# Second MLP: where the last factor's product, the first MLP's last matmuls and the second half's blocks stand in the queues

## The chip, the cores and the metric

One core of one Trainium2 chip. Five instruction queues run beside each other: TensorE (PE; its weight loads are listed as PEld), VectorE (DVE), ScalarE (ACT), GpSimd (POOL) and SyncE (SP), which only issues DMAs. Each queue works its own instructions strictly in the order of the program, and waits where one needs a result of another queue. The metric is the device time of one launch in microseconds; the median of the runs is given. One profiled execution stands beside them.

## The reference, cut to what matters

```python
x = attention(q, k, v)                    # windowed attention with block summaries, x is 1536 x 512
h = x @ w_in                              # first MLP, 512 -> 2048
y = (h * sigmoid(h)) @ w_out              # y is 1536 x 512
a = y @ w_a;  b = y @ w_b                 # second MLP, 512 -> 1536 each
out = (a * b) @ w_out2                    # 1536 x 512
```

Every large product is made of three matmuls on a high and a low part of each operand (high·high, high·low, low·high). The high part is a copy rounded to fp32r, the low part is the rest. So each operand costs one copy (on ACT in most places) and one subtraction (on DVE or POOL) before PE can use it.

## The kernel before, in words

The order of all instructions is written out by hand (`manual_schedule`); nothing is planned by costs. Attention and the first MLP run first, woven into each other. The change touches the passage from the first MLP to the second, and the second MLP.

**End of the first MLP.** A slot of the loop is `mm1` (h), `chain1` (silu and its two parts) and `mm2` of two slots before. When the loop ends, `mm2` of the last two slots is still to be done: eight calls `mm2_part(i, c)` of three matmuls each (L551). The last four finish the four pieces of y for tokens 1024 to 1535, and `keep_y` copies each from PSUM: pieces 0 and 2 on DVE, 1 and 3 on ACT.

**Second MLP.** Tokens are in two halves, q = 0 (tokens 0 to 767) and q = 1 (768 to 1535). The products y·w_a and y·w_b are done with a seven-product (Winograd) scheme on 2 x 2 blocks. A *unit* u is a pair of weight tiles, even u for w_a and odd u for w_b; a *pair* p is units 2p and 2p+1. Of y, each half needs seven blocks, each with a high part (`high_y`, an ACT copy 128x768) and a low part (`low_y`, 128x768): B11, B21 and B22 as they are, and T3 = B22 − B12, T1 = B12 − B11, T2 = T3 + B11, T4 = B21 − T2, which `sum_y` makes in place in the same buffers, so that T3 waits for the parts of B22, T2 overwrites B11 and waits for T1, and so on. For half 0 this is done within the loop; for half 1 the list `second_y` holds the 18 steps, each with its engine.

**A group.** `group(parts, chunks, fills, later)` walks through the seven `PRODUCTS` (k = 0 to 6), and for each k through its parts (unit, half, bank pair). One product is six matmuls of 384 columns (L750) into one of two PSUM banks A and B: k = 0, 2, 4, 6 go to A and k = 1, 3, 5 to B, and k = 2, 3, 5, 6 add onto what is there. After each product come, in this order: `after_product`, then the entries of `later` that are due, then `chunks`, then `fills` of that place in the group. The bank pair of the first part is called bankh in the trace, that of the second bankg. A product that writes a bank has to wait until the instruction that reads the bank's former content is done.

**after_product.** k = 0 copies A to t1 (ACT, L699); k = 1 and 3 make u2 and u3 from B and t1 (DVE, L701, L703). k = 2, 4, 5, 6 finish one of the four factor blocks `at`. For an even unit it is written (ACT L710 or DVE L712). For an odd unit it is multiplied: k = 2 in one instruction (DVE L715), the others with the *bank sum* `x = ps + x` (DVE, L718), which releases the bank, and then the product `at = x * at` (L719), on POOL for k = 4 and 5 and on DVE for k = 6. The rest goes to `later` with a number of products to wait: a DMA of the factor to DRAM (the spill, L725), and for half 0 the high part (`hi`, ACT L733), which in turn puts the low part (`lo`, DVE L737) two products later.

**Order of the groups.** First `[(0, 0, 0), (1, 0, 1)]`: units 0 and 1 of half 0, 14 products in alternation. Into its first places the eight `mm2_part` calls are put, two after each of the first four products, and `second_y` into places 4 to 13. Then nine output matmuls, then unit 0 of half 1 (7 products), then unit 1 of half 1. After that each unit u = 2 to 11 is one group of 14 products, half 0 and half 1 in alternation, with the output matmuls of the pair before (`mm5`, L775, named o in the trace) as chunks and the preparation of the next weights as fills. At places 0 and 1 of an even unit's group stand the two parts of two tiles of w_out2 (`high_wo2` on ACT, `low_wo2` on POOL, L495), which the output matmul at place 4 reads first. At the end `later` is emptied, the last pair's output matmuls follow, and then 288 output matmuls of the other row blocks (L796).

Of the kernel before, what the change touches and what calls it, by code (L numbers as in the profile page):

```python
# [14 lines left out]
ALU = mybir.AluOpType  # L15
# [66 lines left out]
def attention_then_two_mlps(ctx, tc, q, k, v, w_in, w_out, w_a, w_b, w_out2, out):  # L82
# [3 lines left out]
    nc = tc.nc  # L86
# [17 lines left out]
    TH = PT // 2  # L104
# [38 lines left out]
    engines = {"v": nc.vector, "p": nc.gpsimd}  # L143
# [505 lines left out]
    def weights(u, part, i, j):  # L649

        if u % 2:
            assert j == i + 1
            return beside[7 * part + i][:, None, :]
        if u not in wab_t:
            wab_t[u] = pools["w"].tile([P, 2, 7, 2 * P], F32R, tag="wab", name=f"wab{u}", bufs=1)
        return wab_t[u][:, part, i:j]
# [12 lines left out]
    def sum_y(q, name, engine):  # L669
        x, y, op = SUMS[name]  # L670
        engines[engine].tensor_tensor(y_of(q, name), y_of(q, x), y_of(q, y), op=op)
# [9 lines left out]
    def high_y(q, name, h):  # L681
        yc_t[q, name] = [h, None]
        nc.scalar.copy(h, y_of(q, name))

    def low_y(q, name, l, engine):
        h, x = yc_t[q, name][0], y_of(q, name)
        yc_t[q, name][1] = l
        engines[engine].tensor_tensor(l, x, h.bitcast(F32), op=ALU.subtract)

    def spill_of(f):  # L690
        if f not in spill_p:
            spill_p[f] = dram.tile([P, NDEF * P], F32, name=f"spp{f}")
        return spill_p[f]

    def after_product(u, k, q, n, later):
        p, w = divmod(u, 2)
        (A, B), (t1, u2, u3) = banks[n], post["t"][3 * n:3 * n + 3]
        if k == 0:
            nc.scalar.copy(t1, A)  # L699
        elif k == 1:  # L700
            nc.vector.tensor_tensor(u2, B, t1, op=ALU.add)  # L701
        elif k == 3:
            nc.vector.tensor_tensor(u3, B, t1, op=ALU.add)  # L703
        else:

            i, t, ps, x = {2: (0, 0, A, None), 4: (1, 1, A, u3), 5: (1, 0, B, t1), 6: (0, 1, A, u2)}[k]
            at = post["a"][4 * q + 2 * i + t]
            if w == 0:
                if x is None:
                    nc.scalar.copy(at, ps)  # L710
                else:
                    nc.vector.tensor_tensor(at, ps, x, op=ALU.add)  # L712
                return
            if x is None:
                nc.vector.tensor_tensor(at, ps, at, op=ALU.mult)  # L715
            else:

                nc.vector.tensor_tensor(x, ps, x, op=ALU.add)  # L718
                engines["v" if k == 6 else "p"].tensor_tensor(at, x, at, op=ALU.mult)  # L719
            f = 2 * p + i  # L720
            if q or t:

                c = slice(0 if q else P, TH)
                to = q * PT + t * TH + c.start - NOW * P
                later.append((2, lambda: nc.sync.dma_start(spill_of(f)[:, to:to + TH - c.start], at[:, c])))  # L725
            if not q:
                n = P if t else TH

                def hi():
                    if t and (p, "t") not in p_t:  # L730
                        p_t[p, "t"] = work.tile([P, 2, 2, P], F32R, tag="g", name=f"p{p}_t", bufs=3)
                    p_t[p, i, t] = p_t[p, "t"][:, i] if t else work.tile([P, 2, TH], F32R, tag="g", name=f"p{p}_{i}", bufs=3)
                    nc.scalar.copy(p_t[p, i, t][:, 0], at[:, 0:n])  # L733
                    later.append((2, lo))

                def lo():
                    nc.vector.tensor_tensor(p_t[p, i, t][:, 1], at[:, 0:n], p_t[p, i, t][:, 0].bitcast(F32), op=ALU.subtract)  # L737
                later.append((2 if k in (4, 5) else 1, hi))

    def group(parts, chunks, fills, later):  # L740


        at = 0
        for k, (s, y, b, more) in enumerate(PRODUCTS):
            for u, q, n in parts:
                A, B = banks[n]
                idx = 0
                for c in range(2):
                    for a, m in PARTS:
                        nc.tensor.matmul((A, B)[b], weights(u, a, s, s + 1)[:, 0, c * P:(c + 1) * P], yc_t[q, y][m][:, c, :],  # L750
                                         start=(idx == 0 and not more), stop=(idx == 5), skip_group_check=more)
                        idx += 1
                now = [f for x, f in later if x <= 1]
                later[:] = [(x - 1, f) for x, f in later if x > 1]
                after_product(u, k, q, n, later)
                for f in now + chunks.get(at, []) + fills.get(at, []):
                    f()
                at += 1
# [43 lines left out]
    with tc.manual_schedule():  # L802
# [128 lines left out]
        def high_2(name):  # L931
            return lambda: high_y(1, name, places.pop(0))

        def low_2(name, engine):
            return lambda: low_y(1, name, places.pop(0), engine)

        def sum_2(name, engine):
            return lambda: sum_y(1, name, engine)

        second_y = [high_2("B11"), high_2("B22"), low_2("B11", "v"), high_2("B21"), low_2("B22", "p"), sum_2("T3", "v"),  # L940
                    sum_2("T1", "p"), low_2("B21", "p"), sum_2("T2", "v"), high_2("T2"), high_2("T3"), low_2("T2", "v"),
                    sum_2("T4", "p"), high_2("T1"), low_2("T3", "v"), high_2("T4"), low_2("T1", "p"), low_2("T4", "p")]

# [12 lines left out]
        def call(f, *a):  # L956
            return lambda: f(*a)

        def spread(steps, first, last):

            r = {}
            for i, f in enumerate(steps):
                r.setdefault(first + i * (last - first + 1) // len(steps), []).append(f)
            return r

        def merged(*parts):
            r = {}
            for x in parts:
                for k, v in x.items():
                    r.setdefault(k, []).extend(v)  # L970
            return r

        def chunks_of(p):
            return [call(mm5, p, i, t) for i, t in ((0, 0), (0, 1), (0, 2), (1, 3), (1, 0), (1, 1), (1, 2), (0, 3))]
# [4 lines left out]
        def split_wo2(p):  # L979
            return [call(high_wo2, 2 * p), call(low_wo2, 2 * p)], [call(high_wo2, 2 * p + 1), call(low_wo2, 2 * p + 1)]  # L980
# [3 lines left out]
        later = []  # L984

        m2 = [call(mm2_part, i, c) for i in (SLOTS - 2, SLOTS - 1) for c in range(NK)]
        f0, f1 = split_wo2(0)
        group([(0, 0, 0), (1, 0, 1)], {0: m2[0:2], 1: m2[2:4], 2: m2[4:6], 3: m2[6:8]},
              merged({0: f0 + [call(load_unit, 2)], 1: f1}, spread(second_y, 4, 13)), later)
        c = chunks_of(0)  # L990
        for f in c[0:3]:
            f()
# [5 lines left out]
        for u in range(2, UNITS):  # L998
            p, w = divmod(u, 2)
# [5 lines left out]
            if w == 0:  # L1005
                c = chunks_of(p - 1) if p > 1 else []
                if p > 1:
                    f0, f1 = split_wo2(p - 1)
# [10 lines left out]
            else:  # L1019
                if dB is not None:  # L1020
                    parts.append({8: [call(decode_tile, dB)], 9: loads[3:4]})
                if p + 1 == PAIRS:
                    f0, f1 = split_wo2(p)
# [56 lines left out]
```

## Time and profile before

| | |
|---|---|
| runs | 642.73, 642.88, 644.02 us; median 642.88 us |
| profiled execution | 644.93 us, of which the span of the trace is 643.2 us |
| mean granted TensorE clock | 0.995 of full speed |
| PE busy | 615.2 us (96%), 3440 instructions |
| DVE, ACT, POOL busy | 409.0, 307.9 and 308.0 us (64%, 48%, 48%) |

Engine rows give the busy time and its share of the span. In a row of the timeline, the first number is the start in us from the span's start, the second the time from the start of the first to the end of the last instruction that the row merges, xN their count, and the bracket the idle time of that engine before it, with what ended it. Matmul ends are modelled: one of 384 columns is shown 0.33 us long, while the next one starts 0.17 us after it.

### The profile page before, as it was taken

Reading aid. Unit: us, or ns where it says so; the run is one execution under the profiler, and the core shown is the slowest. Engines: PE = TensorE matmul, PEld = TensorE weight load, DVE = VectorE, ACT = ScalarE, POOL = GpSimd, SP = SyncE. Lnnn points to the kernel's source line nnn. Section 1 sums busy time; section 2 is a strip of 40 time slices with the busy share of each in tenths; the row PEclk is TensorE's granted clock in tenths of the full one; section 3 lists DMA queues with packets and bytes.
Section 4 is the critical chain, followed back from the end, with each engine's and each line's share of the span. In section 5 each row is a group of like instructions: output and inputs, shape, how many; then the busy total and the mean of one; then the engine's idle time right before and its main releaser. Section 6 shows DMA issues by size and latency. Waiting matters only on the chain.

```text
span 643.2 us, 9778 instructions
## 1 busy us (share of the span) xinstructions
PE 615.2 (96%) x3440; PEld 537.6 (84%) x3440; DVE 409.0 (64%) x768; ACT 307.9 (48%) x680; POOL 308.0 (48%) x277
## 2 busy tenths in 40 slices
PE   6899999899999999999999889999999999999997
PEld 5888877788878888888888879989999998988886
DVE  6999878985752334567676774685867747364211
ACT  4999678848565224545555323242423324224221
POOL 5657666642431502334457556384654838154220
PEclk8999999899999999999999999999999999999999
DMA  9898998653230235675654013554362502258303
GB/s 230 187 228 246 296 269 255 189 162 103 76 74 18 75 99 170 223 217 177 197 196 167 29 50 103 172 168 148 118 210 83 196 28 88 77 180 305 131 12 130
DMA packets 90521, 97.80 MB, mean 152 GB/s; under 512 B 39000, under 2 KB 68440, under 8 KB 90472
## 3 DMA queue, kind: packets, MB, share of 16 engines
q1 hardware_dynamic: 90472, 97.18, 50.2%
q8 instruction: 27, 0.44, 0.3%
q14 instruction: 22, 0.18, 0.1%
HBM read 73.79 MB, written 23.07 MB: 151 GB/s over the span
## 4 chain that ended last, share of the span: by engine, by line
PE 79%; DVE 11%; ACT 6%; issue 2%; DMA 2%; POOL 0%; SPq 0%; ACTq 0%; DVEq 0%
PE y L551 18%; PE h L518 17%; PE bankg L750 12%; PE bankh L750 12%; PE ol L796 10%; PE o L775 4%; PE sc L360 2%; ACT sm L389 1%; PE av L423 1%; DVE p_t L737 1%; DVE ab L719 1%; DVE sum L718 1%; PE pt L409 1%; DMA sp_out<-w_out 1%; DVE u_in L468 1%
## 5 line engine op out<-in xcount | busy, mean ns | idle before, releaser
L518 PE MATMUL h<-x,w_in 128*128 128x512 f32 (+1 forms) x612 | 143.9, 385 | 0.7 <-DVE g L533 0.6
L551 PE MATMUL y<-g,w_out 128*128 128x512 f32 x576 | 141.3, 394 | 0.8 <-DVE w_out L495 0.8
L518 PEld LDWEIGHTS h<-x,w_in 128*128 128x128 f32 x612 | 110.0, 190 | 23.2 <-issue 0.8
L551 PEld LDWEIGHTS y<-g,w_out 128*128 128x128 f32 x576 | 106.8, 188 | 24.1 <-DVE w_out L495 1.3
L495 POOL TENSOR_TENSOR w_out<-re_out,w_out 128x512 fp32r<-128x512 f32 x37 | 52.1, 1409 | 116.1 <-ACT w_out L147 115.7
L796 PE MATMUL ol<-w_out,plh 128*128 128x512 f32 x192 | 59.1, 389 | 0.0
L533 DVE TENSOR_TENSOR g<-h,g 128x512 fp32r<-128x512 f32 x31 | 21.4, 691 | 49.6 <-ACT g L147 49.4
L495 POOL TENSOR_TENSOR w_out<-w_out,w_out 128x512 fp32r<-128x512 f32 x23 | 31.8, 1389 | 34.5 <-ACT w_out L147 31.0
L719 POOL TENSOR_TENSOR ab<-sum,ab 128x384 f32<-128x384 f32 x24 | 28.5, 1193 | 31.2 <-DVE sum L718 31.1
L526 ACT ACTIVATE h<-h 128x512 f32<-128x512 f32 x31 | 18.0, 582 | 51.1 <-PE h L518 51.1
L796 PEld LDWEIGHTS ol<-w_out,plh 128*128 128x128 f32 x192 | 36.0, 188 | 7.5
L533 POOL TENSOR_TENSOR g<-sg,g 128x512 fp32r<-128x512 f32 x17 | 24.4, 1438 | 36.3 <-ACT g L147 13.2
L147 ACT CAST w_out<-re_out 128x512 fp32r<-128x512 f32 x38 | 23.7, 623 | 34.1 <-issue 23.2
L796 PE MATMUL ol<-w_out,pll 128*128 128x512 f32 x96 | 37.3, 389 | 0.0
L788 DVE TENSOR_TENSOR pll<-pl,plh 128x1024 fp32r<-128x1024 f32 x12 | 17.0, 1416 | 30.9 <-ACT plh L787 30.9
L775 PE MATMUL o<-w_out,p 128*128 128x512 f32 x108 | 30.2, 396 | 0.5 <-DVE p L737 0.5
L403 POOL TENSOR_TENSOR sm<-sm,st 128x480 f32<-128x480 f32 x20 | 22.2, 1116 | 15.8 <-DVE st L399 9.7
L472 DVE SCALAR_TENSOR_TENSOR w_out<-w_out,u_out 128x512 uint32<-128x512 uint32 x28 | 27.3, 976 | 3.7 <-ACT w_out L462 2.3
L389 ACT ACTIVATE sm<-sm,st 128x120 f32<-128x120 f32 x76 | 29.1, 395 | 0.1
L495 POOL TENSOR_TENSOR w_in<-w_in,w_in 128x512 fp32r<-128x512 f32 x15 | 21.5, 1437 | 14.3 <-DVE w_in L149 8.1
L750 PE MATMUL bankh<-yhT,wab 128*128 128x384 f32 x96 | 28.2, 334 | 0.0
L639 POOL TENSOR_TENSOR wab<-c,wab 128x768 fp32r<-128x768 f32 x6 | 11.3, 1877 | 34.4 <-ACT wab L636 34.4
(262 smaller groups left out, 1431.3 us busy)
## 6 DMA issues: line engine op xcount, KB each, us to landing
st_out<-in_moe_w_out_dram SPq DMA_DIRECT2D x28, 512.0 KB, 4.6
re_out<-sp_out SPq DMA_DIRECT2D x44, 256.0 KB, 3.0
st_in<-in_moe_w_in_dram SPq DMA_DIRECT2D x16, 512.0 KB, 6.1
sp_out<-w_out SPq DMA_DIRECT2D x28, 256.0 KB, 2.1
st_a<-in_moe_w_a_dram SPq DMA_DIRECT2D x12, 512.0 KB, 4.0
st_b<-in_moe_w_b_dram SPq DMA_DIRECT2D x12, 512.0 KB, 4.1
c<-spu SPq DMA_DIRECT2D x12, 512.0 KB, 4.1
pl<-spp SPq DMA_DIRECT2D x12, 512.0 KB, 4.5
```

The source lines that it names most:

```text
L147: nc.scalar.copy(o, i)
L389: nc.scalar.activation(sm[:, pr, :], sm[:, pr, :], AF.Exp, scale=-1.0, bias=st[:, 0, pr:pr + 1], accum_out=st[:, 1, pr:pr + 1])
L403: engines[engine].tensor_tensor(sm, sm, st[:, 1, :, None].to_broadcast([P, NPR, KK]), op=ALU.mult)
L472: nc.vector.scalar_tensor_tensor(bits, bits, 3, u_t.pop((kind, f)), op0=ALU.logical_shift_left, op1=ALU.bitwise_or)
L495: engine.tensor_tensor(w[:, 1], w32_t[kind, f], w[:, 0].bitcast(F32), op=ALU.subtract)
L518: nc.tensor.matmul(h_ps[i][:, cols], win_t[f][:, a, c * P:(c + 1) * P], x_t[n][:, steps, m, c, :], start=(idx == 0), stop=(idx == 3 * NK - 1))
L533: engines[engine].tensor_tensor(g_t[i][:, 1], sg_t.pop(i), g_t[i][:, 0].bitcast(F32), op=ALU.subtract)
L551: nc.tensor.matmul(y_ps[n, c], wout_t[i][:, a, c * P:(c + 1) * P], g_t[i][:, m, :], start=(f == 0 and (a, m) == (0, 0)), stop=(f == N1 - 1 ...
L719: engines["v" if k == 6 else "p"].tensor_tensor(at, x, at, op=ALU.mult)
L750: nc.tensor.matmul((A, B)[b], weights(u, a, s, s + 1)[:, 0, c * P:(c + 1) * P], yc_t[q, y][m][:, c, :], start=(idx == 0 and not more), sto ...
L775: nc.tensor.matmul(o_ps[t], g[:, a, c:c + P], w[:, m], start=(begins and (a, m) == (0, 0)), stop=(ends and (a, m) == PARTS[-1]))
L796: nc.tensor.matmul(late_o[j], late_p[f][a][:, j * P:(j + 1) * P], wo2_t[N2 + f][:, m], start=(f == 0 and (a, m) == (0, 0)), stop=(f == N2 ...
```

## The change

The factor's product of k = 6 of an odd unit is put into `later` for one product instead of being issued at once. The spill is due after three products instead of two. `hi` of k = 6 is due after two products instead of one (k = 4 and 5 had two before, k = 2 keeps one). The low part of B22 of half 1 is made on DVE instead of POOL. The eight last `mm2_part` calls, the first two w_out2 tiles and the first step of `second_y` come ahead of the first group, and the other 17 steps of `second_y` are spread over its places 0 to 12.

```diff
@@ after_product
                 nc.vector.tensor_tensor(x, ps, x, op=ALU.add)
-                engines["v" if k == 6 else "p"].tensor_tensor(at, x, at, op=ALU.mult)
+
+                def mult():
+                    engines["v" if k == 6 else "p"].tensor_tensor(at, x, at, op=ALU.mult)
+                if k == 6:
+                    later.append((1, mult))
+                else:
+                    mult()
...
-                later.append((2, lambda: nc.sync.dma_start(spill_of(f)[:, to:to + TH - c.start], at[:, c])))
+                later.append((3, lambda: nc.sync.dma_start(spill_of(f)[:, to:to + TH - c.start], at[:, c])))
...
-                later.append((2 if k in (4, 5) else 1, hi))
+                later.append((2 if k > 2 else 1, hi))
@@ the list second_y
-        second_y = [high_2("B11"), high_2("B22"), low_2("B11", "v"), high_2("B21"), low_2("B22", "p"), sum_2("T3", "v"),
+        second_y = [high_2("B11"), high_2("B22"), low_2("B11", "v"), high_2("B21"), low_2("B22", "v"), sum_2("T3", "v"),
                     sum_2("T1", "p"), low_2("B21", "p"), sum_2("T2", "v"), high_2("T2"), high_2("T3"), low_2("T2", "v"),
                     sum_2("T4", "p"), high_2("T1"), low_2("T3", "v"), high_2("T4"), low_2("T1", "p"), low_2("T4", "p")]
@@ the first group
         f0, f1 = split_wo2(0)
-        group([(0, 0, 0), (1, 0, 1)], {0: m2[0:2], 1: m2[2:4], 2: m2[4:6], 3: m2[6:8]},
-              merged({0: f0 + [call(load_unit, 2)], 1: f1}, spread(second_y, 4, 13)), later)
+        for f in f0 + m2[0:4] + f1 + m2[4:8] + [call(load_unit, 2)] + second_y[0:1]:
+            f()
+        group([(0, 0, 0), (1, 0, 1)], {}, spread(second_y[1:], 0, 12), later)
```

## Rows read from the trace of the kernel before

**Rows 1.** Waits of PE from 340 to 575 us: total us, times, longest us.
```profile
PE bankg L750 <- DVE sum L718: 6.6, 5, 2.3
PE bankh L750 <- DVE sum L701: 1.5, 1, 1.5
PE bankh L750 <- DVE ab L712: 1.5, 1, 1.5
PE o L775 <- DVE p L737: 0.5, 1, 0.5
```

**Rows 2.** Timeline of PE around the first group and the next one.
```profile
346.99 0.33 PE L750 MATMUL bankh<-yhB,wab 128*128 128x384 f32 x1
...
356.75 0.33 PE L750 MATMUL bankh<-yhB,wab 128*128 128x384 f32 x1
...
365.94 0.34 PE L750 MATMUL bankh<-yhB,wab 128*128 128x384 f32 x1
368.59 0.44 PE L750 MATMUL bankg<-yhB,yhT 128*128 128x384 f32 x1 [2.31 <-DVE sum L718]
...
373.50 1.32 PE L750 MATMUL bankh<-more_y,wab 128*128 128x384 f32 x6 [1.49 <-DVE ab L712]
...
378.41 3.41 PE L750 MATMUL bankh<-yp,wab 128*128 128x384 f32 x18 [1.50 <-DVE sum L701]
```

**Rows 3.** Timeline of DVE in the same stretch.
```profile
351.26 0.96 DVE L688 TENSOR_TENSOR ylT<-yt,yhT 128x768 fp32r<-128x768 f32 x1 [0.90 <-ACT yhT L683]
...
365.49 2.57 DVE L671 TENSOR_TENSOR yt<-yt 128x768 f32<-128x768 f32 x1
...
373.94 2.11 DVE L719 TENSOR_TENSOR ab<-sum,ab 128x384 f32<-128x384 f32 x1
```

**Rows 4.** Timeline of POOL in the same stretch.
```profile
346.22 1.30 POOL L495 TENSOR_TENSOR w_out<-re_out,w_out 128x512 fp32r<-128x512 f32 x1 [1.73 <-ACT w_out L147]
...
363.31 1.85 POOL L671 TENSOR_TENSOR yt<-yt 128x768 f32<-128x768 f32 x1 [1.07 <-DVE yt L671]
365.11 2.13 POOL L688 TENSOR_TENSOR more<-yt,more_y 128x768 fp32r<-128x768 f32 x1
```

**Rows 5.** Timeline of ACT: the first high parts of half 1.
```profile
358.37 2.31 ACT L683 CAST more_y<-yt 128x768 fp32r<-128x768 f32 x3
```

**Rows 6.** Timeline of PE at the passage from unit 3 to unit 4.
```profile
423.83 0.34 PE L750 MATMUL bankh<-yhB,wab 128*128 128x384 f32 x1
425.24 0.97 PE L750 MATMUL bankg<-more_y,wab 128*128 128x384 f32 x4 [1.07 <-DVE sum L718]
...
429.51 0.86 PE L775 MATMUL o<-w_out,p 128*128 128x512 f32 x3
```

**Rows 7.** Timeline of DVE at the same passage.
```profile
422.10 0.56 DVE L718 TENSOR_TENSOR sum<-bankh,sum 128x384 f32<-128x384 f32 x1 [0.23 <-PE bankh L750]
422.69 1.01 DVE L719 TENSOR_TENSOR ab<-sum,ab 128x384 f32<-128x384 f32 x1
423.63 1.08 DVE L737 TENSOR_TENSOR p_t<-ab,p_t 128x128 fp32r<-128x128 f32 x1
424.64 0.55 DVE L718 TENSOR_TENSOR sum<-bankg,sum 128x384 f32<-128x384 f32 x1
```

**Rows 8.** Timeline of POOL at the same passage.
```profile
421.99 1.30 POOL L639 TENSOR_TENSOR wab<-s,wab 128x512 fp32r<-128x512 f32 x1
423.25 1.32 POOL L719 TENSOR_TENSOR ab<-sum,ab 128x384 f32<-128x384 f32 x1
...
427.10 1.61 POOL L495 TENSOR_TENSOR w_out<-w_out,w_out 128x512 fp32r<-128x512 f32 x1
```

**Rows 9.** The chain of waits after the last unit: start us, us, what.
```profile
567.72 1.20 DVE ab L719
568.91 1.30 DVE p_t L737
...
571.80 2.60 PE o L775 x10
```

## The prediction

> **What bounds the kernel now.** I read the page first: PE is busy for 96% of the span, so only what PE waits for can be won, and no instruction of PE is removed by this change. Then the list of PE's waits for the stretch from 340 to 575 us, in which everything lies that the change moves. The reader sees there eight waits, all ended by DVE [rows 1]. Then the timelines of PE, DVE, POOL and ACT around each, and the chain of waits for the last one. A wait costs a little more than its idle time, since the end of a matmul is shown some 0.16 us after the point at which the next could start: from 365.94 to 368.59 are 2.65 us instead of 0.17, so 2.48 us are lost where the idle time says 2.31 [rows 2]. Counted so, there are three places:
> - the first pair, three waits: 2.48 + 1.66 + 1.67 = 5.8 us [rows 2];
> - the passages from an odd unit to the next even one. Of the five waits for L718 in rows 1 one is the 2.31; the other four make 4.3 us idle, one each after units 3, 5, 7 and 9. At the first, the last matmul starts at 423.83 and the next product at 425.24 instead of 424.00: 1.24 us lost, four times 5.0 [rows 6];
> - one wait after the last unit, 0.46 idle in the timeline (0.5 in the list), 0.6 us lost [rows 1, 9].
> Together 11.4 us. That is the most that the change can give.
>
> **The passages (product of k = 6 behind the other bank sum).** The bankg product waits for its bank sum, which starts at 424.64. In front of it on DVE, after the bankh sum at 422.10, stand the factor product (1.01) and a low part of 128 columns (1.08) [rows 7]. Both have two inputs in SBUF, and both end just behind an instruction of POOL: 422.69 + 1.01 = 423.70 behind 423.29, and 423.63 + 1.08 = 424.71 behind 424.57, so 0.41 and 0.14 us after POOL's end [rows 7, 8]. The bank sums, with one input in PSUM, keep their 0.55 [rows 7]. After the change the low part follows the bankh sum directly, is held until POOL's 423.29 and ends at about 423.43; the bankg sum then runs until 423.9, and PE gets it at 423.95, before its 424.00. The 1.24 us go.
>
> What is late next: the factor product now runs on DVE behind the sum, and the second one behind the next unit's first copy; DVE has the same instructions as before, and nothing of PE waits for these. But the output matmuls at place 4 read a low part that POOL makes at 427.10, for 1.61 us, until 428.71 [rows 8]. POOL's queue up to there is the same as now and does not move. The second of these matmuls starts at 429.51 + 0.23 = 429.74 now, and would start at 428.50 if PE is 1.24 us earlier [rows 6]: about 0.3 us of wait comes back. I take 1.24 − 0.3 = 0.94 for each passage, 3.8 us for the four. Bounds: nothing, if POOL gets later by as much as PE gets earlier, and 5.0 if it gets a bit faster.
>
> **The end.** The same two instructions, 1.20 and 1.30 us long, stand in front of the second bank sum after the last unit [rows 9]. With the product behind that sum, the low part that PE waits for ends at about 571.1 by the same steps, and PE needs it at 571.80 − 0.6 = 571.2. So 0.6 us go, with little to spare (bounds 0 and 0.6). Behind it PE has work without a wait, so an earlier start is an earlier end.
>
> **The first pair.** The eight pieces of the first MLP are 24 matmuls at 0.23 us and take 5.5 us; they run from 346.99 to 352.5 instead of in four portions up to 356.75, and the first products fill the time behind them. PE arrives at k = 2 at the same time as now, 356.7 [rows 2]. Do they lose cover? Their last operand, a low part on POOL, is done at 346.22 + 1.30 = 347.5 and is needed at 349.8 [rows 4]: no wait, cost 0. What moves is y: its last piece is done 4.2 us earlier, so the high parts of half 1 start at about 354.0 instead of 358.37 [rows 2, 5]. DVE is free for the copies of y at 352.2, when the low part of T4 ends [rows 3].
>
> I carry the steps on in the order of each queue. ACT casts come 0.74 apart [rows 5]; a 128x768 step is 0.96 on DVE and 1.85 on POOL when undisturbed [rows 3, 4]; bank sums 0.55, 0.47 apart [rows 7]. Low B11 ends on DVE at 355.8, low B22 at 357.3 between the sums u2, T3 at 358.6, T1 on POOL from 358.7 to 360.5. Moving low B22 to DVE costs 0.9 there and takes about 1.9 from POOL in front of T1; I count it within this chain. T2 on DVE needs T1. It is ready at 360.56, but POOL has started low B21 at 360.5 (it does so now as well: 365.11 against 365.49, and T2 takes 2.57 and ends 0.8 after POOL's end [rows 3, 4]). So T2 ends at 363.1, and the sum u3 behind it at 363.6: product k = 5 of unit 0 starts at 363.65 instead of 362.92, **0.73 lost**. Low T2 is held likewise by T4's sum on POOL (363.2 to 365.05) and ends at 365.85; the factor sum behind it ends at 366.3, and product k = 6 of unit 0 starts at 366.35 instead of 365.73, **0.62 lost**. Then DVE catches up: the sum for which PE waits 2.48 us now is done at 367.25 and is needed at 367.4; the next group's first bank is read by 369.5, needed at 370.5; the sum u2 for its k = 3 is done at 373.4, needed at 373.6. That last margin, 0.2 us, is the thinnest, because the factor product in front of it is held by POOL as it is now (2.11 us at 373.94 [rows 3]). So 1.35 us of new waits for 5.8: a gain of 4.4. Bounds: 5.8 if POOL and DVE miss each other, and 0 if the held steps come back in other places with the same length.
>
> The Trainium skill, "SBUF — State Buffer", section "Who interferes with whom", says that GpSimd and a VectorE instruction with two SBUF inputs exclude each other, and that issue order alone decides which of the two blocks. By this T2 would lose nothing if it were issued before low B21: the 0.73 would go, and the forecast would be 0.7 lower. The rows speak for POOL being first, and a price between the two is within the range.
>
> **Spills and high parts one product later.** A spill is a DMA on SP, whose queue is in order: behind it stand reloads for the next weights, used a group later, so a delay of one product (1.04 us) is hidden by the 14 products in between; one reload even gets ahead of the last spill. The high part of k = 6 is due behind the copy t1 on ACT; its reader is an output matmul more than 14 products on, after the last unit it is the eighth group of output matmuls. I cost both at 0; without the cover it would be 1 us at the end, once.
>
> **Sum.** 4.4 + 3.8 + 0.6 = 8.8 us. The profiled execution has a span of 643.2 and 644.93 us in all, so it would become 636.1. It lies 2.05 above the median of 642.88; taken from that, 634.1 us.
>
> **Rivals.**
> 1. Everything fits: all waits go and none comes back, −11.4: 631.5 us. For it speaks that the margins that I miss are below 0.8 us; against it that POOL has no slack in front of the w_out2 parts.
> 2. The wait changes its place at the passages: POOL's low part of w_out2 gets later and takes the 1.24 us back each time. Then only 4.4 + 0.6 remain: 637.9 us. For it: POOL is busy without a break from 421.99 to 428.7 [rows 8]; against it: what holds POOL there are DVE's two-input steps, whose number is unchanged.
> 3. The first pair gives nothing: DVE, with low B22 added, stays behind, and the holds come back inside the group. −(3.8 + 0.6): 638.5 us. Against it: all these steps start more than 4 us earlier.
> 4. 2 and 3 together, about −0.6: no change, 642.3 us.
> 5. Slower: `second_y` in the places 0 to 12 stands in front of the bank sums on DVE, and each step that POOL holds delays all sums behind it, at about 2.1 us each [rows 3]. To outweigh the 8.8 and be seen, it takes five such holds on PE's path more than in my chain, which has two: 644.5 us or more. Today's 5.8 us are made of holds like these, so the mechanism is real; but their count is not raised by the change.
>
> **Chances.** Forecast 0.60 (its own range 633.0 to 635.8), rival 1 0.10, rival 2 0.12, rival 3 0.08, rival 4 0.05, rival 5 0.05. A change of less than 0.2% (1.3 us) can't be told from none here. So faster 0.90, same 0.05, slower 0.05. The range from 631.4 to 638.2 takes in the forecast and rivals 1 and 2.
>
> **What would show it.** In the timeline of PE: no wait in front of the last product of the first group, the first product of the next and its k = 3, but two waits of 0.5 to 0.8 us in front of k = 5 and k = 6 of unit 0; no wait for L718 at the four passages, but one of about 0.3 us inside the output matmuls at place 4, ended by POOL L495; no wait after the last unit. On DVE: the bankg sum at the passage starts about 1.2 us earlier in relation to the bankh sum. The prediction is wrong if waits of over 1 us at the passages or in the first group remain, or if PE waits ahead of the first group for an operand of the last slots.

## The result, and the profile after

635.81 us median (635.28 to 636.16, 4 runs) against 643.45 us (642.73 to 644.37, 4 runs): a ratio of 0.988, 95% interval 0.9863 to 0.9897. In a second set of runs, on another occasion, it was 633.95 against 643.91, ratio 0.9847 (0.9823 to 0.9872). The kernel is faster by 1.2 to 1.5%; 634.1 us were forecast, with 631.4 to 638.2 as the range.

The list of PE's waits from 340 to 575 us in the profile after (total us, times, longest us) has three lines in place of the four of before [rows 1]:

```profile
PE bankh L756 <- DVE sum L703: 0.7, 1, 0.7
PE bankh L756 <- DVE ab L712: 0.4, 1, 0.4
PE o L781 <- POOL w_out L495: 0.2, 1, 0.2
```

The reader sees that no line with L718 is left: the bank sum that follows a factor product, which ended five of the eight waits, ends none. What has come instead are the sum u3 (L703), the factor sum of unit 0 (L712) and POOL's low part of w_out2.

**The first pair.** The timeline of PE after: the last y matmuls stand together (24 of the 27 in the row are those behind the loop, from 346.47), the two waits are in front of k = 5 and k = 6 of unit 0, and the next group starts at 370.31 without a wait (before: 373.50, and two waits beside it [rows 2]).

```profile
345.79 6.29 PE L551 MATMUL y<-g,w_out 128*128 128x512 f32 x27
...
363.20 0.45 PE L756 MATMUL bankh<-yhT,wab 128*128 128x384 f32 x1 [0.70 <-DVE sum L703]
...
366.02 0.44 PE L756 MATMUL bankh<-yhB,wab 128*128 128x384 f32 x1 [0.44 <-DVE ab L712]
...
370.31 1.23 PE L756 MATMUL bankh<-more_y,wab 128*128 128x384 f32 x6
```

DVE after, in the same stretch: T3, T2, the two sums u3 behind it, low T2 and the factor sum behind that, then the factor product and the sum u2 of the next group. T2 still takes 2.58 us, now from 360.10 instead of 365.49 [rows 3].

```profile
357.13 0.95 DVE L671 TENSOR_TENSOR yt<-yt 128x768 f32<-128x768 f32 x1
...
360.10 2.58 DVE L671 TENSOR_TENSOR yt<-yt 128x768 f32<-128x768 f32 x1 [1.10 <-POOL yt L671]
362.60 0.54 DVE L703 TENSOR_TENSOR sum<-bankh,sum 128x384 f32<-128x384 f32 x1
...
363.58 1.92 DVE L688 TENSOR_TENSOR yp<-yt,more 128x768 fp32r<-128x768 f32 x1
365.42 0.55 DVE L712 TENSOR_TENSOR ab<-bankh,sum 128x384 f32<-128x384 f32 x1
...
369.86 2.19 DVE L721 TENSOR_TENSOR ab<-sum,ab 128x384 f32<-128x384 f32 x1
372.68 0.56 DVE L701 TENSOR_TENSOR sum<-bankh,sum 128x384 f32<-128x384 f32 x1 [0.63 <-PE bankh L756]
```

POOL after: T1, low B21, T4's sum. Each held DVE's neighbour: T2 ends 0.8 us after low B21, low T2 0.8 us after T4's sum.

```profile
358.22 1.84 POOL L671 TENSOR_TENSOR yt<-yt 128x768 f32<-128x768 f32 x1 [4.13 <-DVE yt L671]
360.03 1.83 POOL L688 TENSOR_TENSOR more<-yt,more_y 128x768 fp32r<-128x768 f32 x1
362.82 1.86 POOL L671 TENSOR_TENSOR yt<-yt 128x768 f32<-128x768 f32 x1 [0.96 <-DVE yt L671]
```

**The passage from unit 3 to unit 4.** DVE after: the bankg sum starts at 418.30, 1.25 us behind the bankh sum; before it was 2.54 [rows 7].

```profile
417.05 0.56 DVE L718 TENSOR_TENSOR sum<-bankh,sum 128x384 f32<-128x384 f32 x1 [0.24 <-PE bankh L756]
417.52 0.85 DVE L743 TENSOR_TENSOR p_t<-ab,p_t 128x128 fp32r<-128x128 f32 x1
418.30 0.54 DVE L718 TENSOR_TENSOR sum<-bankg,sum 128x384 f32<-128x384 f32 x1
418.77 0.90 DVE L721 TENSOR_TENSOR ab<-sum,ab 128x384 f32<-128x384 f32 x1
```

PE after: the bankg product follows at 418.96, 0.18 us behind the matmul before it, and three output matmuls last 1.27 instead of 0.86 us [rows 6].

```profile
418.78 0.34 PE L756 MATMUL bankh<-yhB,wab 128*128 128x384 f32 x1
418.96 1.27 PE L756 MATMUL bankg<-more_y,wab 128*128 128x384 f32 x6
...
423.19 1.27 PE L781 MATMUL o<-w_out,p 128*128 128x512 f32 x3
```

POOL after: the low part of w_out2 that they wait for ends at 423.68, inside the three.

```profile
422.08 1.60 POOL L495 TENSOR_TENSOR w_out<-w_out,w_out 128x512 fp32r<-128x512 f32 x1
```

**Where the time went**, by the starts on PE in the two timelines: the stretch from PE's first instruction behind the loop (346.99 before, 346.47 after) to the first matmul of L796, now L802 (574.24 and 564.44) was 227.2 us and is 218.0: 9.3 us less.

| part of this stretch | before | after | won | forecast |
|---|---|---|---|---|
| up to the first product of unit 1, half 1 | 36.42 | 31.90 | 4.5 | 4.4 |
| units 4, 6, 8, 10, from first product to the next unit's | 3 x 20.23, 20.25 | 3 x 19.36, 18.89 | 4.0 | 3.8 |
| the last pair's output matmuls | 6.27 | 5.48 | 0.8 | 0.6 |

The starts show more than the list of waits. Units 4, 6 and 8 each take 0.47 us longer than unit 10, while the list names one wait of 0.2 us for all three; in e6 below the list is empty, and these units take 19.35 to 19.41 us all the same.

### The profile page after: what moved, and what is told of

Its sections match the earlier page's. It is cut to its first block, busy times and chain, and to the rows that moved or that the text cites. A ratio compares the mean times of both kernels' runs of the same rounds, so it can differ in the third digit from the quotient of the medians.

```text
span 633.6 us, 9781 instructions
## 1 busy us (share of the span) xinstructions
PE 612.9 (97%) x3440; PEld 536.2 (85%) x3440; DVE 409.2 (65%) x769; ACT 307.9 (49%) x680; POOL 307.7 (49%) x276
## 4 chain that ended last, share of the span: by engine, by line
PE 72%; DVE 10%; ACT 7%; POOL 4%; issue 3%; DMA 3%; SPq 0%; ACTq 0%; DVEq 0%; POOLq 0%
PE y L551 17%; PE h L518 15%; PE bankg L756 11%; PE ol L802 10%; PE bankh L756 10%; PE o L781 5%; DMA sp_out<-w_out 2%; ACT sm L389 2%; POOL wab L639 1%; PE av L423 1%; POOL ab L721 1%; POOL w_out L495 1%; DVE w_in L472 1%; PE sc L360 1%; DVE u_in L468 1%
## 5 line engine op out<-in xcount | busy, mean ns | idle before, releaser
L518 PE MATMUL h<-x,w_in 128*128 128x512 f32 (+1 forms) x612 | 142.3, 382 | 1.0 <-DVE g L533 0.6
L802 PE MATMUL ol<-w_out,plh 128*128 128x512 f32 x192 | 59.2, 390 | 0.0
L802 PEld LDWEIGHTS ol<-w_out,plh 128*128 128x128 f32 x192 | 36.0, 188 | 7.7 <-POOL w_out L495 0.3
L802 PE MATMUL ol<-w_out,pll 128*128 128x512 f32 x96 | 37.4, 389 | 0.0
L468 DVE TENSOR_SCALAR u_out<-st_out 128x512 uint32<-128x512 uint32 x28 | 26.1, 934 | 0.0
```

The source lines that it names most:

```text
L468: nc.vector.tensor_scalar(u, t[:, :, 0], 29, None, op0=ALU.logical_shift_right)
L518: nc.tensor.matmul(h_ps[i][:, cols], win_t[f][:, a, c * P:(c + 1) * P], x_t[n][:, steps, m, c, :], start=(idx == 0), stop=(idx == 3 * NK - 1))
L802: nc.tensor.matmul(late_o[j], late_p[f][a][:, j * P:(j + 1) * P], wo2_t[N2 + f][:, m], start=(f == 0 and (a, m) == (0, 0)), stop=(f == N2 ...
```

## The experiments

Each starts from the changed kernel if nothing else is said. *Stretch* is the 218.0 us just described. In the profiles of this study its start lies anywhere from 344.9 to 348.2 us, while its length repeats within 0.1 us for the same kernel, and what follows it is 69.0 to 69.1 us in all; so differences of a few tenths are read from the stretch, and the ratio to the kernel before stands beside it.

**e1: the product at once again.**

```diff
-                if k == 6:
-                    later.append((1, mult))
-                else:
-                    mult()
+                mult()
```

> Undoes one part of the change: the factor's product of k = 6 is issued at once again, in front of the other half's bank sum; the rest of the change stays. My theory (the product and a low part stood in front of the bank sum for which PE waits): the four waits for L718 at the passages come back with 1.24 us each, the 0.37 us inside the output matmuls go, and the 0.6 to 0.8 us after the last unit come back, so 4.2 to 4.8 us slower than the changed kernel and about 4 us faster than the kernel before. Rival (the gain at the passages comes from the later spills and high parts, which relieve SP and ACT there): no waits for L718, time as the changed kernel, within 0.5 us.

640.2 us, ratio 0.9933 (0.9909 to 0.9957), stretch 222.7: 4.7 us longer. Four waits for L718 are back (4.3 us idle in all), the last pair's matmuls take 6.24 us, no wait for POOL is left. DVE at the passage has the old order and the old times, and PE's bankg product the old wait:

```profile
416.20 0.56 DVE L718 TENSOR_TENSOR sum<-bankh,sum 128x384 f32<-128x384 f32 x1 [0.23 <-PE bankh L753]
416.79 1.00 DVE L721 TENSOR_TENSOR ab<-sum,ab 128x384 f32<-128x384 f32 x1
417.71 1.09 DVE L740 TENSOR_TENSOR p_t<-ab,p_t 128x128 fp32r<-128x128 f32 x1
418.73 0.55 DVE L718 TENSOR_TENSOR sum<-bankg,sum 128x384 f32<-128x384 f32 x1
```
```profile
419.33 0.98 PE L753 MATMUL bankg<-more_y,wab 128*128 128x384 f32 x4 [1.07 <-DVE sum L718]
```

So the deferral makes the 4.8 us of passages and end, within 0.1 us; the rival is out (and e4 takes the two delays away and loses nothing).

**e2: the last y matmuls and the steps of half 1 at their old places.**

```diff
-        for f in f0 + m2[0:4] + f1 + m2[4:8] + [call(load_unit, 2)] + second_y[0:1]:
-            f()
-        group([(0, 0, 0), (1, 0, 1)], {}, spread(second_y[1:], 0, 12), later)
+        group([(0, 0, 0), (1, 0, 1)], {0: m2[0:2], 1: m2[2:4], 2: m2[4:6], 3: m2[6:8]},
+              merged({0: f0 + [call(load_unit, 2)], 1: f1}, spread(second_y, 4, 13)), later)
```

> Undoes another part alone: the first MLP's last matmuls go back into places 0 to 3 of the first group and the 18 steps of second_y to places 4 to 13; the deferred product, the later spills and low B22 on DVE stay. My theory (the steps of half 1 start 4 us too late, DVE cannot catch up): the three waits of 2.5, 1.7 and 1.7 us around the first group come back, perhaps 0.4 us shorter because low B22 is off POOL, and the two waits for k = 5 and 6 go; 4.0 to 4.6 us slower than the changed kernel. Rival (it was low B22 on POOL that held T3 and all behind it, and the places matter little): at most 2 us slower than the changed kernel.

639.26 us, ratio 0.9915 (0.989 to 0.9939), stretch 222.2: 4.3 us longer. PE waits again, 2.0 us in front of the last product of the first group (before: 2.3) and 1.5 in front of k = 3 of the next; the third line of the list is the wait for POOL's w_out2 part, as in the changed kernel:

```profile
PE bankg L756 <- DVE sum L718: 2.0, 1, 2.0
PE bankh L756 <- DVE sum L701: 1.5, 1, 1.5
```

The third, in front of the next group, is there too, though no idle time shows it. In this execution the granted clock fell to 0.50 (the lower level, 1.2 GHz) from 367.60 to 370.80 us and was 1.00 up to 367.40 and from 371.00. It fell shortly after the wait of 2.0 us; the first profile of the kernel before has such a wait too and no such spell. The nine output matmuls there take 3.80 us instead of 2.25:

```profile
367.43 3.80 PE L781 MATMUL o<-w_out,p 128*128 128x512 f32 x9
371.14 1.31 PE L756 MATMUL bankh<-more_y,wab 128*128 128x384 f32 x6
```

They fill the time of the wait. On DVE the factor sum that frees the bank ends at 370.54 + 0.55 = 371.09, and the group starts at 371.14, 4.88 us behind the first wait's end as it was 4.91 before. So the slow spell cost nothing, and the places are worth 4.3 us. The first wait is 0.3 us shorter than before; that may be low B22, which is off POOL here, but was not tried apart.

**e3: low B22 on POOL.** `low_2("B22", "v")` becomes `low_2("B22", "p")`.

> Undoes one engine: low B22 of half 1 on POOL again, all else as changed. My theory (undisturbed it is 1.85 us on POOL against 0.95 on DVE, and POOL has free time in front of it): T3 starts some 0.2 to 0.9 us later, and the waits in front of k = 5 and k = 6 of unit 0 grow by 0.2 us in all, at most 1: as the changed kernel within 0.5 us. Rival of e2 (low B22 on POOL is what held the first pair): 2 us or more slower than the changed kernel.

635.05 us, ratio 0.9842 (0.9817 to 0.9866), stretch 217.6: 0.3 us *shorter*, within the 0.5 us that I allowed and of the other sign. POOL makes low B22 from 354.97 in time that is free, and DVE has one step less in front of T3; the wait in front of k = 5 goes from 0.70 to 0.35 us.

```profile
354.97 1.98 POOL L688 TENSOR_TENSOR more_y<-yt,more_y 128x768 fp32r<-128x768 f32 x1 [0.54 <-ACT more_y L683]
```
```profile
PE bankh L756 <- DVE ab L712: 0.5, 1, 0.5
PE bankh L756 <- DVE sum L703: 0.4, 1, 0.4
```

The move of low B22 to DVE is thus a small loss at the new places, about 0.3 us.

**e4: spills and high part as before.** `(3, …)` becomes `(2, …)` for the spill, and `2 if k > 2 else 1` becomes `2 if k in (4, 5) else 1` for `hi`.

> Undoes the two delays alone: spills due after two products again, the high part of k = 6 after one; the deferred product stays, so both now stand right behind it. My theory (both are off PE's path): as the changed kernel within 0.3 us, the same waits of PE in the trace. Rival (an ACT or SP queue held by the wait for the later product, with the copy t1 and the reloads behind it): a wait of PE for t1 at each passage, up to 1 us each, up to 4 us slower than the changed kernel.

635.66 us, ratio 0.9855 (0.983 to 0.9881), stretch 218.03 against 217.97 and 218.00: no difference. Both delays cost and bring nothing.

**e5: the first output matmul one place later.** `enumerate((4, 6, 8, 10, 11, 12))` becomes `enumerate((5, 6, 8, 10, 11, 12))`.

> The changed kernel with one number changed: the first output matmul of a pair stands at place 5 of the even unit's group instead of 4, one product (1.04 us) further behind the w_out2 part that POOL makes. My theory (PE waits there 0.37 us for POOL's low part, at three of the four passages): these waits go and nothing else changes, 1.1 us faster than the changed kernel. Rival (POOL is the bound at the passages, so that the wait moves on to the next thing that POOL makes): as the changed kernel within 0.3 us.

634.31 us, ratio 0.9838 (0.9818 to 0.9857), stretch 216.7: 1.3 us shorter. Units 4, 6 and 8 take 18.95 us instead of 19.36, and the output matmuls are back at their length:

```profile
422.58 0.86 PE L781 MATMUL o<-w_out,p 128*128 128x512 f32 x3
```

**e6: T2 behind the sums.** The steps are listed by place (-1 is ahead of the group), and the group takes this list in place of the spread one:

```diff
+        second_y = {-1: [high_2("B11")], 0: [high_2("B22"), low_2("B11", "v")], 1: [high_2("B21")], 2: [low_2("B22", "v")],
+                    3: [sum_2("T3", "v"), sum_2("T1", "p")], 4: [low_2("B21", "p")], 6: [high_2("T3")],
+                    7: [sum_2("T2", "v")], 8: [high_2("T2")], 9: [sum_2("T4", "p"), high_2("T1"), low_2("T3", "v")],
+                    10: [low_2("T2", "v")], 11: [high_2("T4"), low_2("T1", "p")], 12: [low_2("T4", "p")]}
```

> The changed kernel with the steps of half 1 in other places: T2 on DVE at place 7 instead of 5, behind the two sums u3 that it held up; low T2 at 10 instead of 7, T4's sum at 9 instead of 8, with the high parts of T2 and T4 at 8 and 11. Same instructions, same engines. My theory (PE waits for bank sums that stand behind T2 and low T2 on DVE, and these are held by POOL): both waits, in front of k = 5 and k = 6 of unit 0 (0.86 and 0.6 us lost), go, and a new one of 0 to 0.4 us comes in the next group: 1.0 to 1.5 us faster than the changed kernel. Rival (DVE has too much work in the first group, whatever the order): the waits only move, as the changed kernel within 0.3 us.

632.67 us, ratio 0.9828 (0.9807 to 0.9849), stretch 216.3: 1.6 us shorter. Both waits of the first group are gone and no new one came; up to the first product of unit 1, half 1, PE takes 30.16 us instead of 31.90. That is a little more than expected.

**e7: e5 and e6 together.**

> e5 and e6 together. My theory: both gains add, 2.1 to 2.6 us faster than the changed kernel, about 1.5% faster than the kernel before, and PE has no wait of over 0.3 us between the first pair and the last row blocks. Rival: as the better of the two alone.

631.89 us, ratio 0.981 (0.979 to 0.983), stretch 215.0: 3.0 us shorter than the changed kernel (1.3 + 1.6 = 2.9). The list of PE's waits from 340 to 575 us is empty, and the starts agree: 30.14 us up to unit 1 of half 1, and 18.95 to 18.97 for units 4, 6 and 8. This version beats both kernels. Its T2, two places later, meets less of low B21, and no wait stands behind it:

```profile
362.64 1.75 DVE L671 TENSOR_TENSOR yt<-yt 128x768 f32<-128x768 f32 x1
```

**e8: the kernel before, a second profile**, unchanged.

> The kernel before once more, for a second profile. The two profiles say 9.65 us between before and after, the medians of the runs 7.64. If the difference lies in the stretch before the change (a spell of lower granted clock in one execution), this profile has 227.2 us again from the first of the last y matmuls or products (346.99) to the first matmul of the last row blocks, and another length ahead of it. If the waits of the kernel before differ from execution to execution, the stretch itself is 1 to 2 us shorter here.

Stretch 227.2 again (from 347.43 to 574.65). The list has seven of the eight waits, with the same lengths within 0.03 us. The one in front of the next group is covered as in e2: the granted clock was 0.50 from 370.50 to 373.70, the nine output matmuls take 3.80 us, and the group starts 4.88 us behind the first wait's end (369.02 to 373.90). So the waits are the same in both executions of this program, and what differs between the two lies ahead of the stretch.

**e9: low B21 on DVE, behind T2.** T2 and its high part move up one place by this.

```diff
-                    sum_2("T1", "p"), low_2("B21", "p"), sum_2("T2", "v"), high_2("T2"), high_2("T3"), low_2("T2", "v"),
+                    sum_2("T1", "p"), sum_2("T2", "v"), high_2("T2"), high_2("T3"), low_2("B21", "v"), low_2("T2", "v"),
```

> The changed kernel with low B21 of half 1 on DVE, just ahead of low T2, instead of on POOL ahead of T2. Now POOL has nothing to do while T2 runs. My theory (DVE and POOL hold each other whole instructions long, and it was low B21 on POOL that made T2 2.58 us long): T2 takes 0.95 us, the wait in front of k = 5 of unit 0 goes; low T2 now meets T4's sum on POOL and takes 2.3 us, so that the wait in front of k = 6 of unit 0 grows from 0.6 to about 1.4 us, and one of 0.1 to 0.2 may show in front of k = 4 of unit 1. In all as the changed kernel, within 0.5 us. Rival (T2 is long of itself, or held by something on ACT or by PSUM): T2 stays above 2 us and the wait in front of k = 5 gets longer by the 0.9 us that low B21 adds to DVE.

635.16 us, ratio 0.986 (0.9839 to 0.9882), stretch 218.2. With POOL idle T2 takes 0.96 us; low T2, which now meets T4's sum on POOL (362.65 to 364.50), takes 2.42:

```profile
359.75 0.96 DVE L671 TENSOR_TENSOR yt<-yt 128x768 f32<-128x768 f32 x1 [2.01 <-POOL yt L671]
...
362.89 2.42 DVE L688 TENSOR_TENSOR yp<-yt,more 128x768 fp32r<-128x768 f32 x1
```
```profile
PE bankh L756 <- DVE ab L712: 1.2, 1, 1.2
```

The wait for k = 5 is gone, that for k = 6 is 1.2 us idle. The 1.6 us of T2 were POOL's doing. In the sum they came back: low B21 itself takes 0.95 us on DVE in front of low T2, and low T2 is 0.5 us longer at its meeting with POOL.

**e10: the changed kernel again**, unchanged.

> The changed kernel once more, to weigh the 9.3 us by which the stretch after the loop is shorter in the profiles against the 7.6 us by which the medians of the first runs differ. If what differs between executions lies ahead of that stretch, the stretch is again 217.97 us from the first of the last y matmuls to the first matmul of the last row blocks, and the difference of the medians comes nearer to 9.3 (8 to 10). If the kernel gives less outside of the profile, it stays at 7 to 8.

633.95 against 643.91 us, 10.0 apart, stretch 218.00. This fits the 9.3 us of the profiles: by its interval the second set has 8.2 to 11.4 us, the first 6.6 to 8.8. That the first set falls short by the scatter of what comes ahead of the stretch is likely, but not shown, since executions without a trace do not tell where their time went.

## Why the prediction was right, point by point

- **The passages.** Right in mechanism and nearly in size. The two instructions in front of the bank sum make PE's next product 1.24 us late; with the product deferred the sum is in time (418.96, no wait), although the low part of 128 columns still stands there. e1 brings the whole back. The wait for POOL's w_out2 part came where it was forecast, at 0.41 us (20.23 to 19.36 won 0.87, e5 won 0.41 more) instead of 0.3. At the fourth passage, where the prediction counted it too, it did not come: there POOL starts that part 2.7 us into unit 10 instead of 4.2 into unit 4, so PE kept 1.36 us. Together 4.0 instead of 3.8.
- **The end.** 0.8 instead of 0.6: its wait is gone too, as e1 shows by bringing it back.
- **The first pair.** Right in nearly every step. T3 to T2 came 5 us earlier; T2 was held by low B21 on POOL, low T2 by T4's sum; the two new waits cost 0.86 and 0.60 us where 0.73 and 0.62 were worked out, and the three old ones went (e2). The margin of 0.2 us in front of k = 3 held, but for another reason than the one worked out: DVE was through with the held factor product 0.63 us before it could start the sum u2 (372.68), which waited for PE's own product. Cover lost ahead of the first group: none, the y matmuls run without a wait.
- **Who blocks.** The Trainium skill, "SBUF — State Buffer", section "Who interferes with whom", has GpSimd and a two-SBUF-input VectorE instruction lock each other out by issue order. The trace agrees: POOL's 360.03 came ahead of DVE's 360.10, by 0.07 us, and DVE paid 1.6 us; e9 took the POOL instruction away and T2 was 0.96 us. The wait that the prediction hung on the order of the two, 0.73 us, was 0.86; no run puts T2 first and low B21 behind it on POOL, but in e9 this wait is gone.
- **Low B22 on DVE.** The one step that I counted without weighing it by itself. I took POOL's 1.9 us in front of T1 as the thing to be saved; at the new places that time is free, and DVE is what T3 waits for. It costs 0.3 us (e3).
- **Spills and high part.** 0, as forecast (e4).
- **The sum.** 8.8 us were forecast for a stretch that gave 9.3. Both sides of the sum were too small. A wait was priced up to its end, but the matmul that ends it loses time as well: from 368.59 [rows 2] to the next start are 0.27 us instead of 0.17, and behind each of the eight waits the second matmul is late by about as much:

```profile
368.86 0.34 PE L750 MATMUL bankg<-ylB,yhT 128*128 128x384 f32 x1
```

The eight waits were therefore worth 12.5 us, not 11.4: 36.42 − 30.14 = 6.3 in the first pair (against e7, which has no wait there), 1.36 at each passage (read at unit 10), 0.8 at the end. The new ones took 31.90 − 30.14 = 1.8 and three times 19.36 − 18.89 = 0.47 (of which e5 takes 0.41 away), together 3.2 where 2.55 were forecast. So 11.4 was not the most that can be won: e7 wins 12.2.
- **The time.** It came out at 635.81 instead of 634.1, at the upper edge of the forecast's own 633.0 to 635.8, although the stretch gave more than forecast. The 2.05 us by which the profiled execution lay above the median of before were taken as fixed. The start of the stretch differs by up to 3.3 us between profiles, and the same kernel gave 633.95 in the second set; where in this band a median of four runs falls is chance.

## What to carry to other kernels

Put what frees a bank ahead of what only uses the result, across both halves of a double-buffered loop: one instruction moved past another half's read was worth 4.7 us (e1). When work is moved to a place where PE has lost it as a cover, walk the in-order queues with the measured durations; two engines that lock each other need their meetings listed one by one, because a hold taken away at one place can come back in part at the next (e9). A step behind which reads of PSUM queue up belongs behind those reads, even if it can start earlier (e6).

## What I had not expected

The length of the stretch repeats to 0.1 us from execution to execution (227.24 and 227.23; 217.97 and 218.00), while its start moves between 344.9 and 348.2 us for code that is the same in all kernels. A part goes with the clock: in six of the twelve profiles the granted clock between 100 and 200 us is 0.98, and their stretch starts at 346.1 to 348.2; in the other six it is 1.00, and the start is at 344.9 to 346.5. What moves the rest was not tried and stays open. The mean clock of a whole profile says little of it: the second profile of the kernel before has 0.989, but one of its slow spells lies inside the stretch, where it cost nothing (e8). For the comparison of schedules a profile's stretch tells tenths where medians of four to six runs tell one or two microseconds.
